# A gated loop and a feed-forward layer on one core: fp32 weight pieces, no selecting products for three pairs, and a new order table

## The chip, the core and the metric

The kernel runs on one core of a Trainium2 chip. A core has five engines that work in parallel and meet only through semaphores: PE (TensorE, matrix products), ACT (ScalarE), DVE (VectorE), POOL (GpSimd) and SP (SyncE, which here only issues DMA transfers). Each takes its instructions strictly in order. The metric is the device time of one execution in microseconds (us), as the median of several runs.

## The reference

There are 4 sequences of 768 steps with 8 heads of 48 columns. The first part is a linear attention whose state decays and turns by a complex gate a at each step. Its output, 384 columns a step, goes through a layer norm and a feed-forward layer:

```python
mag = np.sqrt(a_re * a_re + a_im * a_im)
scale = np.minimum(mag, 0.999) / (mag + 1e-06)
a_re_n, a_im_n = (a_re * scale, a_im * scale)
for t in range(S):
    new_re = ar * S_re - ai * S_im
    new_im = ar * S_im + ai * S_re
    kv = np.einsum('bhd,bhe->bhde', k[:, :, t], v[:, :, t])
    S_re, S_im = (new_re + kv, new_im)
    y[:, :, t] = np.einsum('bhd,bhde->bhe', q[:, :, t], S_re)
...
xn = (x - mu) / np.sqrt(var + 1e-06) * g_ln
ch = np.maximum(xn @ w_ch1, 0.0) @ w_ch2       # 384 -> 1536 -> 384
return (x + ch).astype(np.float32)
```

## The kernel before

**Tiling.** Steps are taken in chunks of 128, two chunks to a pair, so there are 12 pairs, three to a sequence. The pairs 0, 3, 6 and 9 are the first of their sequences. Pair 0 is done in two halves of four heads.

**Work of a pair.** From a_re and a_im come the logarithm of the gate's size (`ln`, `iv`, `r`, `r2`, `u`, `l`, `lc`) and its angle (`th`). Products with a triangle of ones (`u_e`, and `u_th`, which holds 1/2π) sum them over the steps: `dec` for the sizes, `ph` for the angles in turns. `e` and `en` are the exponentials of the sums; `sin` and `cos` come from the low 16 bits of the phase, with `abs` or `qt` on the way. `ke`, `ks`, `qe`, `qs` multiply k and q by them. `ksT` and `qsT` are their transposes: PE transposes into a bank and ACT or DVE copies it out, or SP does the whole with a transposing DMA. Then come the masked products within the chunk (`am`, `atm`), the state (`gm`, `gs`, `G`), the output `y`, the norm's figures (`bn`, `rstd`), the centred rows `x` and their transpose (`xtr`, `xT`), the feed-forward products `mm1`, `relu`, `mm2`, and the result `ot` (with `oa` where ACT takes a part of it), stored by `st`.

**Carried phase.** `ph` begins with a product of `pick`, a matrix that selects rows of `car`. `car` holds the phase at the end of the pair before it; for a sequence's first pair it is the constant 192 (`WINDOW`), which keeps the sum in a range whose low 16 bits are the fraction of a turn.

**Weights.** `wl.0` and `wl.1` are two casting DMAs from POOL's queue, each for a whole weight matrix (fp32 in memory, bf16 on the chip: `w1b`, `w2b`). `wc` then multiplies `w1b` in place by minus the norm's gain, in nine pieces of 512 columns, and `mm1` needs these, `mm2` needs `wl.1`.

**Order.** A long table, `PLAN`, written out by hand or by a planner, lists each step with its engine (P, A, V, G, S) and the PSUM bank. The kernel emits the steps in that order; the table is therefore each engine's order too. An `@` puts a step of POOL behind a step of DVE. The `warm` steps are products on `u_e` whose results nobody reads. `RINGS` gives the number of buffers of each kind: a step that writes a buffer waits for the readers of the step that many places before.

Of the kernel before, what the change touches and what calls it, by code (L numbers as in the profile page):

```python
# [20 lines left out]
TWO_PI_SAFE = 6.2831845  # L21
PSUM = bass.MemoryType.PSUM
# [15 lines left out]

OPTIONAL = ("kT", "qT", "xtr", "oa", "ac", "tab", "warm", "xr", "ks", "qs", "ke", "qe")
# [25 lines left out]
xtr.0:P4 kT.3:P6 ksT.2:V7 ph.2.0:P2 G.1:V0 qe.2.0.1:G@ksT.2 tab.trig.5:A th.3.0:A ksT.3:V6 am.2:P0 ngl:G@ksT.2
sin.2.0:A2 warm.w37:P7 v.1:G atm.2:V0 warm.13:P7 am.3:P6 xT.0:A4 qt.2.0:P2 r2.3.0:G@ksT.3 x.1:A5 gm.2:P4 atm.3:V6
ph.3.0:P0 cos.2.0:A2 xr.0:G G.2:V4 warm.23:P2 are.5.0:S xtr.1:P2 car.3.0:A0 warm.9:P3 warm.w41:P6 sin.3.0:A0 gm.3:P4
wc.0.1:V y.2:P7 wc.1.0:V y.3:P5 xT.1:A2 wc.1.1:V wc.1.2:V vf.2.0:S qt.3.0:P0 wl.1:G@wc.1.1 bn.2:V7 mm1.0.1.0:P2
cos.3.0:A0 wc.0.0:V mm1.0.1.1:P2 vf.2.1:S wc.0.2:V x.2:A7 wc.2.2:V mm1.0.0.1:P0 wc.2.0:V relu.0.1:A2 wc.2.1:V bn.3:V5
mm1.0.0.0:P0 qe.2.0.0:G@wc.2.1 xtr.2:P3 aim.5.0:S x.3:V5 mm1.0.2.0:P6 ke.2.0.0:G@bn.3 xT.2:V3 xtr.3:P5 mm1.0.2.1:P6  # L70
xT.3:V5 tab.log.6:A u.3.0:A gs.3:V4 mm1.1.0.1:P2 qs.2.0.0:V relu.0.2:A6 mm1.1.1.0:P4 ks.2.0.0:V relu.0.0:A0
mm1.1.1.1:P4 ks.2.0.1:V mm1.1.0.0:P2 l.3.0:V ln.4.0:A mm1.1.2.1:P0 relu.1.1:A4 relu.1.0:V2 kT.5:P6 mm1.1.2.0:P0
iv.4.0:A ksT.5:V6 qT.5:P4 relu.1.2:A0 lc.3.0:V qT.4:P3 r.4.0:G@ksT.5 qsT.5:V4 kT.4:P5 qsT.4:A3 dec.3.0:P6 ksT.4:V5
# [141 lines left out]
def kernel(  # L215
# [62 lines left out]
    def eng(name):  # L278
        return g.ops[name].eng
# [583 lines left out]
```

## Time and profile before

| what | value |
|---|---|
| device time, 3 runs | median 186.26 us (185.86 to 186.31) |
| span of the profiled execution | 184.4 us, from its first to its last instruction |
| that execution's own time | not given apart from the runs; 186.26 − 184.4 = 1.9 us lie around the span |
| busy: PE, DVE, ACT, POOL | 175.1, 154.5, 154.9, 111.2 us |
| of PE, warming products | 14.6 us (42 of 512 columns) and 7.1 us (29 of 256) |
| DMA | 35.39 MB in 128791 packets; SP's queue 84.3% and POOL's 7.0% of 16 engines' span |

A row of grouped instructions reads: line, engine, operation, output <- input, shape, count | busy us, mean ns of one | idle time of the engine before them and who ended it. PE's products are pipelined and their ends are modelled, so the durations of neighbours overlap and a busy PE need not be at its peak.

### The profile page before, as it was taken

To read this page: it belongs to the slowest core of one execution; us is meant where nothing else is said; L and a number is where in the kernel's file an instruction comes from. 1 tells how busy PE (TensorE), PEld (TensorE's weight loads), DVE (VectorE), ACT (ScalarE), POOL (GpSimd) and SP (SyncE) were. 2 spreads that over 40 slices of the span, in tenths; PEclk is the share of its full clock that TensorE was granted. 3 is DMA by queue.
4 is the path that set the end of the run, shared out by engine and by line. 5 is a ranking of instruction groups with operands and counts; after the bars stand their busy time and mean duration, and the time that the engine had idled before them with its cause. 6 is when DMAs were issued, how large, how long until landed. Compare 5 with 4: busy or idle time off the path is not lost.

```text
span 184.4 us, 5011 instructions
## 1 busy us (share of the span) xinstructions
PE 175.1 (95%) x1971; PEld 138.2 (75%) x1971; DVE 154.5 (84%) x273; ACT 154.9 (84%) x217; POOL 111.2 (60%) x124
## 2 busy tenths in 40 slices
PE   5968989999999999999999999999999999999992
PEld 2545367789866886987887897887977979788871
DVE  2349999998888999999989989988988999977431
ACT  5899988989999999999999999999989973466320
POOL 7484068942586847799799966877959530280000
PEclk9999999999999999999999999999999999999999
DMA  5999999999986999989896999989699999992302
GB/s 142 305 201 230 231 187 187 231 252 203 231 176 138 252 256 217 197 222 198 183 242 126 229 221 191 214 187 215 148 233 165 207 135 201 242 199 90 108 0 85
DMA packets 128791, 35.39 MB, mean 192 GB/s; under 512 B 124800, under 2 KB 128000, under 8 KB 128768
## 3 DMA queue, kind: packets, MB, share of 16 engines
q1 hardware_dynamic: 127968, 32.72, 84.3%
q0 software_dynamic: 800, 2.36, 7.0%
q8 instruction: 15, 0.25, 0.5%
q14 instruction: 8, 0.07, 0.1%
HBM read 28.31 MB, written 4.72 MB: 179 GB/s over the span
## 4 chain that ended last, share of the span: by engine, by line
PE 74%; DVE 10%; SPq 7%; DMA 4%; issue 2%; POOL 1%; DVEq 0%
PE banks L767 24%; PE banks L791 23%; PE banks L613 6%; PE banks L636 5%; SPq L452 3%; SPq L404 3%; PE banks L507 3%; PE banks L488 3%; PE banks L697 2%; PE banks L660 2%; PE banks L700 2%; DMA k<-in_k_dram 2%; PE banks L734 2%; DMA q<-in_q_dram 2%; DVE qs L295 1%
## 5 line engine op out<-in xcount | busy, mean ns | idle before, releaser
L791 PE MATMUL banks<-w2b,h 128*128 128x384 bf16 (+2 forms) x300 | 53.0, 319 | 0.1
L767 PE MATMUL banks<-xT,w1b 128*128 128x256 bf16 x432 | 51.5, 273 | 0.0
L767 PEld LDWEIGHTS <-w1b 128*128 128x128 bf16 x432 | 46.1, 114 | 1.1 <-DVE stats L707 0.3
L779 ACT ACTIVATE h<-banks 128x1024 bf16<-128x1024 f32 x31 | 31.5, 1021 | 11.5 <-PE banks L767 11.3
L791 PEld LDWEIGHTS <-h 128*128 128x128 bf16 x300 | 26.9, 97 | 13.8 <-issue 0.2
L295 DVE TENSOR_TENSOR atm<-banks,mask 128x1024 bf16<-128x1024 f32 x24 | 28.9, 1219 | 3.6 <-PE banks L636 3.3
L295 POOL TENSOR_TENSOR r<-aim,are 128x768 f16<-128x768 f32 x9 | 16.5, 1832 | 8.6 <-DVE ksT L292 7.5
L831 ACT ACT_TABLE_LOAD x15 | 19.2, 1283 | 1.0 <-PEq L847 0.8
L295 POOL TENSOR_TENSOR qe<-q,e 128x384 bf16<-128x384 f32 (+1 forms) x14 | 16.2, 1157 | 4.7 <-ACT e L492 1.7
L826 PE MATMUL banks<-u_e 128*128 128x512 f16 x42 | 14.6, 436 | 2.4 <-POOL u_e L323 2.2
L724 POOL TENSOR_SCALAR xr<-x,mv 128x384 f32<-128x384 bf16 x13 | 8.5, 653 | 11.0 <-ACT x L714 4.7
L707 DVE BATCH_NORM_STATS2 stats<-banks 128x6 f32<-128x384 f32 x24 | 13.3, 556 | 1.2 <-PE banks L700 1.2
L636 PE MATMUL banks<-qsT,ksT 128*128 128x128 bf16 x192 | 14.3, 219 | 0.0
L477 DVE SCALAR_TENSOR_TENSOR l<-r,w 128x768 f16<-128x768 f16 (+1 forms) x13 | 11.7, 907 | 2.6 <-ACT r L473 2.6
L807 DVE SCALAR_TENSOR_TENSOR ot<-banks,rstd,xr 128x384 f32<-128x384 f32 (+2 forms) x18 | 10.4, 586 | 3.9 <-PE banks L791 3.3
L636 PEld LDWEIGHTS <-ksT 128*128 128x128 bf16 x192 | 12.2, 97 | 1.6 <-DVE ksT L292 0.2
L414 POOL TENSOR_SCALAR v<-vf 128x768 bf16<-128x768 f32 x9 | 9.5, 1058 | 5.6 <-DVE mv L708 2.7
L805 POOL TENSOR_TENSOR ot<-ot,x 128x384 f32<-128x384 f32 x7 | 7.0, 1006 | 9.1 <-DVE atm L295 7.9
L697 PE MATMUL banks<-v,atm 128*128 128x48 bf16 x192 | 12.0, 183 | 0.2 <-DVE atm L295 0.2
L459 ACT ACTIVATE w<-are 128x768 f32<-128x768 f32 (+1 forms) x13 | 10.2, 791 | 2.2 <-DMA are<-in_a_re_dram 2.2
L295 POOL TENSOR_TENSOR ke<-k,en 128x768 bf16<-128x768 f32 (+1 forms) x9 | 11.8, 1321 | 0.2
L697 PEld LDWEIGHTS <-atm 128*128 128x128 bf16 x192 | 10.8, 96 | 1.4 <-DVE atm L295 0.6
(100 smaller groups left out, 391.0 us busy)
## 6 DMA issues: line engine op xcount, KB each, us to landing
vf<-in_v_dram SPq DMA_DIRECT2D x24, 192.0 KB, 3.0
q<-in_q_dram SPq DMA_DIRECT2D x24, 192.0 KB, 3.8
k<-in_k_dram SPq DMA_DIRECT2D x24, 192.0 KB, 3.8
out_dram<-ot SPq DMA_DIRECT2D x23, 192.0 KB, 2.3
are<-in_a_re_dram SPq DMA_DIRECT2D x8, 384.0 KB, 4.6
aim<-in_a_im_dram SPq DMA_DIRECT2D x8, 384.0 KB, 5.0
are<-in_a_re_dram SPq DMA_DIRECT2D x8, 192.0 KB, 4.7
aim<-in_a_im_dram SPq DMA_DIRECT2D x8, 192.0 KB, 3.8
```

The lines of the kernel that those rows point to most:

```text
L295: {"DVE": nc.vector, "POOL": nc.gpsimd}[eng(name)].tensor_tensor(**kw)
L477: nc.vector.scalar_tensor_tensor(out=S_("l"), in0=S_("r2"), scalar=0.5, in1=S_("w"), op0=ALU.mult, op1=ALU.add)
L613: nc.tensor.transpose(ps[:, h], T(nm, P)[:, c, h], ident)
L636: nc.tensor.matmul(ps[:, h], lhsT=T("ksT", n)[:, h], rhs=T("qsT", n)[:, h], start=True, stop=True)
L697: nc.tensor.matmul(ps[:, h], lhsT=T("atm", n)[:, h], rhs=T("v", P)[:, c, h], start=True, stop=nfirst)
L707: nc.vector.bn_stats(out=T("stats", n), in_=bank(f"y.{n}")[:, 0:DM])
L767: nc.tensor.matmul(ps[:, jj], lhsT=w1b[:, dc, ts(gi, JG * C)].rearrange("k (p j) -> k j p", j=JG)[:, jj], rhs=T("xT", P)[:, dc].rearrange( ...
L779: act(out=dst, in_=src, func=AF.Relu)
L791: nc.tensor.matmul(bank(f"o.{N}")[:, ws], lhsT=T("h", P)[:, j, ts(c, C)], rhs=w2b[:, j, ws], start=(j == 0), stop=(j == NJ - 1))
L807: nc.vector.scalar_tensor_tensor(out=o, in0=bank(f"o.{N}")[:, ws], scalar=T("rstd", P)[:, ds(c, 1)], in1=xs, op0=ALU.mult, op1=ALU.add)
L826: g.add(f"warm.w{i}", lambda i=i: nc.tensor.matmul(bank(f"warm.w{i}"), lhsT=u_e[:, 0, 0], rhs=u_e.rearrange("p c j t -> p (c j t)"), start ...
L831: g.add(f"tab.{nm}.{i}", lambda tab=tab: nc.scalar.preload_act_table_set(tab))
```

## The change

**Weights.** `wl.0` and `wl.1` are gone. SP issues 18 transfers of [128, 512] fp32 (`ws.0` to `ws.8` for w_ch1, `ws.9` to `ws.17` for w_ch2) into a ring of two buffers `ws`. Nine steps `wc` scale a piece into `w1b`, nine steps `wd` cast one into `w2b`. In the new table two `wc` and one `wd` are on DVE, two and two on ACT, five and six on POOL. `mm2` of a group of four row blocks needs the three pieces `wd` of that group.

**First pairs of sequences 1 to 3.** For pairs 3, 6 and 9, `ph` has no product of `pick`. A new step `root` writes 1206 (192 turns in radians, nearly) over the first step's angle instead, in one partition.

**Order table.** All of `PLAN` is new. Engines change with it: relu goes from 31 on ACT and 5 on DVE to 24 and 12, `oa` from 7 to none, ksT on ACT from none to 5, transposes of x by DMA from 2 to 6; the warming products become 60 of 512 columns and 9 of 256.

SP's queue, where the loads of pairs 4 to 6 stand (are, aim, k, q and vf are a_re, a_im, k, q and v; the number is the buffer). Before:

```order
L452 DMA are_65<-in_a_re_dram 128x8x96
L452 DMA aim_68<-in_a_im_dram 128x8x96
L452 DMA are_66<-in_a_re_dram 128x8x96
L404 DMA vf_76<-in_v_dram 128x8x48 x2
L452 DMA aim_69<-in_a_im_dram 128x8x96
L452 DMA are_64<-in_a_re_dram 128x8x96
L404 DMA q_70<-in_q_dram 128x8x48
L592 DMA row_166<-e_98 8x1x48
```

After:

```order
L401 DMA ws_168<-in_moe_w_ch_dram 128x512
L425 DMA vf_76<-in_v_dram 128x8x48 x2
L401 DMA ws_167<-in_moe_w_ch_dram 128x512
L473 DMA are_66<-in_a_re_dram 128x8x96
L401 DMA ws_168<-in_moe_w_ch_dram 128x512
L473 DMA are_64<-in_a_re_dram 128x8x96
L401 DMA ws_167<-in_moe_w_ch_dram 128x512
L473 DMA aim_69<-in_a_im_dram 128x8x96
L401 DMA ws_168<-in_moe_w_ch_dram 128x512
L473 DMA aim_67<-in_a_im_dram 128x8x96
```

The loads of are and aim of pairs 5 and 6 now stand between pieces of w_ch2, each of which waits for a cast.

ACT's queue around the last pair's exponentials (L492, then L513), which is where the first products of pair 8's feed-forward stand. Before:

```order
L831 ACT_TABLE_LOAD
L473 ACTIVATE r_88<-r_88 128x768
L290 COPY qsT_123<-banks 128x1024
L779 ACTIVATE h_158<-banks 128x1024
L714 ACTIVATE x_139<-banks,mv_149 128x384
L796 ACTIVATE ot_160<-banks,mv_147,rstd_152 128x384
L779 ACTIVATE h_158<-banks 128x1024 x2
L492 ACTIVATE e_98<-banks 128x768
L492 ACTIVATE en_100<-banks 128x768
```

After:

```order
L859 ACT_TABLE_LOAD
L778 ACTIVATE rstd_153<-mv_148 128x2
L779 ACTIVATE rstd_153<-rstd_153 128x2
L513 ACTIVATE e_98<-banks 128x768
L513 ACTIVATE en_100<-banks 128x768
L294 COPY ksT_116<-banks 128x1024
L742 ACTIVATE x_139<-banks,mv_149 128x384
L807 ACTIVATE h_158<-banks 128x1024 x2
```

The exponentials now stand ahead of pair 8's three relu (h_158), and a copy of ksT is ahead of them too.

PE's queue at the phase of pair 3 (th is the angle). Before:

```order
L503 LDWEIGHTS pick
L503 MATMUL banks<-car_164,pick 128x384
L507 LDWEIGHTS u_th
L507 MATMUL banks<-th_93,u_th 128x384
L507 LDWEIGHTS u_th
L507 MATMUL banks<-th_93,u_th 128x384
```

After:

```order
L534 LDWEIGHTS u_th
L534 MATMUL banks<-th_93,u_th 128x384
L534 LDWEIGHTS u_th
L534 MATMUL banks<-th_93,u_th 128x384
```

Each of the pair's two chunks has lost its product of `pick`. The code (of the table, one line of each; the rest is left out):

```diff
+ROOT_RAD = 1206.0
-         "mv": 5, "rstd": 5, "xT": 3, ...
+         "mv": 5, "ws": 2, "rstd": 5, "xT": 3, ...
+ROOT = {3, 6, 9}
...
-ue:G are.0.0:S are.1.0:S are.0.1:S uth:V aim.0.0:S warm.w27:P0 pad.ks.2:G warm.1:P0 aim.0.1:S pad.qs.2:G warm.w1:P7
+ue:G are.0.0:S aim.0.0:S car0.1:G uth:V warm.w0:P0 warm.w1:P0 one:G are.0.1:S zrow.0:G warm.w2:P0 zrow.1:G pad.qs.2:G
...
+              "row": ([C, HALF], BF16), "ws": ([C, 512], FP32), ...
...
-    g.add("wl.0", lambda: nc.gpsimd.dma_start(
-        out=w1b, in_=moe_w_ch1.rearrange("(dc p) j -> p dc j", p=C)))
-    g.add("wl.1", lambda: nc.gpsimd.dma_start(
-        out=w2b.rearrange("p (g j) e -> p g (j e)", j=JG),
-        in_=moe_w_ch2.rearrange("(g p j) e -> p g (j e)", p=C, j=JG)))
...
-    def f_wc(jb, ec):
-        w, sc, name = w1b[:, ec, ts(jb, 512)], ngl[:, ds(ec, 1)], f"wc.{jb}.{ec}"
-                out=w, in0=w, scalar1=sc, scalar2=None, op0=ALU.mult)
+    def f_wc(i, name, dst, sc):
         if eng(name) == "ACT":
+            nc.scalar.mul(out=dst, in_=T("ws", i), mul=sc)
         else:
+                out=dst, in0=T("ws", i), scalar1=sc, scalar2=None, op0=ALU.mult)
+    def f_wd(i, name, dst):
+        if eng(name) == "ACT":
+            nc.scalar.copy(out=dst, in_=T("ws", i))
+        else:
+                out=dst, in0=T("ws", i), scalar1=1.0, scalar2=0.0, op0=ALU.mult, op1=ALU.add)
+    for m in range(2):
+        for a in range(NG):
+            for b in range(ND):
+                i = (m * NG + a) * ND + b
+                src = w2d[:, a, ts(b, 512)] if m else moe_w_ch1[ts(b, C), ts(a, 512)]
+                g.add(f"ws.{i}", lambda i=i, src=src: nc.sync.dma_start(out=T("ws", i), in_=src),
+                      uses=[("ws", i)])
...
+            if P in ROOT:
+                def f_root(X=X, hs=hs, step=step):
+                    {"DVE": nc.vector, "POOL": nc.gpsimd}[eng(f"root.{X}")].memset(
+                        step(T("th", P), 0)[0:1], ROOT_RAD)
...
-                    nc.tensor.matmul(ps[:, c], lhsT=pick[rows], rhs=T("car", P)[rows, fs],
+                    if P not in ROOT:
+                        nc.tensor.matmul(ps[:, c], lhsT=pick[rows], rhs=T("car", P)[rows, fs],
...
-                                         start=False, stop=end,
+                                         start=(P in ROOT and j == 0), stop=end,
...
-                        needs=[f"relu.{P}.{part}", "wl.1"] + ...
+                        needs=[f"relu.{P}.{part}"] + [f"wd.{part}.{x}" for x in range(ND)] + ...
...
-    for i in range(29):
+    for i in range(9):
         g.add(f"warm.{i}", ...
-    for i in range(42):
+    for i in range(60):
         g.add(f"warm.w{i}", ...
```

More of the change, by code (lines that the diff above doesn't have):

```diff
@@ L65 @@
[L65 to L73, printed above, removed]
-are.6.0:S am.5:P0 e.3.0:A6 rstd.0:G am.4:P2 atm.5:V0 r2.4.0:A mm2.0.0:P4 mm2.0.1:P4 atm.4:V2 u.4.0:A q.3.0:S
@@ new lines @@
+mm1.2.0.1:P0 root.6.0:V st.2:S abs.5.0:V6 v.3:G@ks.3.0.0 q.5.1:S kT.7:P5 sin.5.0:A6 qs.3.0.0:V gm.6:P2 q.4.0:S kT.6:P4
+G.6:A2 mm1.2.0.0:P0 cos.5.0:A ksT.7:V5 v.4:G@qs.3.0.0 qT.7:P7 ksT.6:V4 relu.2.0:A0 qT.6:P6 ke.4.0.0:G@qs.3.0.0
+are.7.0:S qsT.7:V7 gm.7:P2 dec.5.0:P3 cos.4.0:A G.7:V2 am.7:P0 qsT.6:V6 r2.6.0:A vf.5.0:S ks.4.0.0:G mm2.4.0:P2
+atm.7:V0 am.6:P6 vf.5.1:S mm2.4.1:P2 atm.6:V6 y.7:P0 tab.log.8:A e.5.0:A3 aim.7.0:S mm2.5.0:P1 qe.4.0.0:G bn.7:V0
+en.5.0:A3 y.6:P6 mm2.4.2:P2 bn.6:V6 vf.6.0:S x.7:A0 gm.8:P7 ln.7.0:A ot.4:V2 xtr.7:P3 rstd.3:G kT.9:P5 k.5.0:S
```

205 lines of the change are left out of this document (110 added, 95 removed), and 2 rows, old and new, of the table RINGS.

## The prediction

> **What bounds the kernel now.** I read the page first, then three stretches, then the groups by shape, then the queues.
>
> ```profile
> span 184.4 us, 5011 instructions
> ...
> PE 175.1 (95%) x1971; PEld 138.2 (75%) x1971; DVE 154.5 (84%) x273; ACT 154.9 (84%) x217; POOL 111.2 (60%) x124
> ...
> ACT  5899988989999999999999999999989973466320
> ...
> PEclk9999999999999999999999999999999999999999
> DMA  5999999999986999989896999989699999992302
> ```
>
> The runs' median is 186.26 us, so 1.9 us lie around this execution's span; every sum below is a change of the span, carried over to the median. The clock is at nine tenths or more in every slice and leaves the sums. The slices say that ACT is as full as PE from 10 to 145 us and then nearly idle. So I cut the span at the first product of pair 0's feed-forward and at that of pair 8:
>
> ```profile
> 38.52 2.81 PE L767 MATMUL banks<-xT,w1b 128*128 128x256 bf16 x24
> ...
> 59.86 2.78 PE L767 MATMUL banks<-xT,w1b 128*128 128x256 bf16 x24
> ...
> 142.72 1.47 PE L767 MATMUL banks<-xT,w1b 128*128 128x256 bf16 x12
> ```
> ```profile
> 0.00:37.00 37.00, 31.31 (x278) 19.54 (x279) 27.31 (x51) 32.49 (x51) 22.90 (x40) 1.00 0.99 214
> 37.00:142.70 105.70, 105.65 (x1260) 86.56 (x1259) 97.36 (x175) 102.05 (x138) 78.43 (x73) 1.00 0.98 204
> 142.70:184.40 41.70, 38.18 (x437) 32.10 (x434) 29.83 (x49) 20.32 (x30) 9.88 (x12) 1.00 0.71 141
> ```
>
> The columns are the stretch, then PE, PEld, DVE, ACT, POOL, clock, share of the DMA engines, GB/s. In the middle PE lacks 0.05 us, ACT 3.6 us, DVE 8.3 us. In the last 41.7 us PE goes on alone and ACT is half idle. So PE is the bound after 37 us, but ACT stands 3.6 us behind it: an order that asks ACT for more than that before 142.7 us makes ACT the bound. ACT's one large wait, for the feed-forward's sums (11.3 us in all), lies mostly in the tail:
>
> ```profile
> ACT h L779 <- PE banks L767: 11.3, 14, 1.8
> ```
>
> **Selecting products gone.** Pairs 3, 6 and 9 lose two products each. Their pitch is the time to the next product, 0.16 us:
>
> ```profile
> 32.48 0.33 PE L503 MATMUL banks<-car,pick 128*128 128x384 f16 x1
> 32.65 0.49 PE L507 MATMUL banks<-th,u_th 128*128 128x384 f16 x2
> 32.97 0.33 PE L503 MATMUL banks<-car,pick 128*128 128x384 f16 x1
> ```
>
> 6 × 0.16 = 1.0 us off PE, on its busy part. Three fills of one row (root) come in, one on DVE and two on POOL, each like this one:
>
> ```profile
> L359 POOL MEMSET qrow<- 1x384 f16 x1 | 0.4, 411 | 0.1
> ```
>
> 0.4 us each on engines with idle time; nothing on the sum. The new order also drops 4 of 22 xtr groups of three 128-column products (by columns 4 × 0.16 = 0.6 us). PE's total falls by 1.6 us.
>
> **Weights.** The two casting transfers and the nine in-place scalings go; 18 pieces of 256 KB, nine scalings and nine casts from fp32 come.
>
> ```profile
> L385 DVE TENSOR_SCALAR w1b<-w1b,ngl 128x512 bf16<-128x512 bf16 x9 | 2.5, 345 | 0.0
> L724 POOL TENSOR_SCALAR xr<-x,mv 128x384 f32<-128x384 bf16 x13 | 8.5, 653 | 11.0 <-ACT x L714 4.7 <-DVE mv L708 1.7 <-DVE qe L295 1.7
> L414 POOL TENSOR_SCALAR v<-vf 128x768 bf16<-128x768 f32 x9 | 9.5, 1058 | 5.6 <-DVE mv L708 2.7 <-DVE xT L292 1.8 <-DVE ks L295 0.6
> L290 ACT COPY xT<-banks 128x384 bf16<-128x384 bf16 x6 | 2.9, 476 | 1.9 <-PE banks L734 1.8
> L412 ACT CAST v<-vf 128x768 bf16<-128x768 f32 x3 | 2.5, 822 | 0.0
> ```
>
> DVE keeps three pieces (0.345 each if fp32 costs nothing, 0.7 if it doubles; I take 0.5): 1.5 for the old nine's 2.5. POOL takes eleven, each between 0.65 and 1.06 us, by width 0.8: 8.8 us, which its 40% of idle time hides if the pieces are there. ACT takes four, between 0.48 and 0.82, by width 0.6: 2.4 us, with no cover, since ACT is full.
>
> **The moved work, on ACT.** Counting the table up to the first product of pair 8, with the mean of each kind:
>
> ```profile
> L779 ACT ACTIVATE h<-banks 128x1024 bf16<-128x1024 f32 x31 | 31.5, 1021 | 11.5 <-PE banks L767 11.3
> L542 ACT ACTIVATE sh<-banks 128x768 f16<-128x768 int16 x6 | 4.8, 808 | 0.0
> L796 ACT ACTIVATE ot<-banks,mv,rstd 128x384 f32<-128x384 f32 x7 | 4.7, 671 | 0.3 <-PE banks L791 0.3
> L290 ACT COPY dec<-banks 64x8 f32<-64x8 f32 x12 | 1.9, 156 | 0.6 <-PE banks L597 0.4
> L290 ACT COPY qsT<-banks 128x1024 bf16<-128x1024 bf16 x3 | 3.0, 1004 | 0.5 <-PE banks L613 0.5
> L714 ACT ACTIVATE x<-banks,mv 128x384 bf16<-128x384 f32 x14 | 8.0, 581 | 3.1 <-PE banks L700 2.4 <-DVE mv L708 0.5
> L750 ACT ACTIVATE rstd<-mv 128x2 f32<-128x2 f32 x2 | 0.4, 207 | 0.0
> L751 ACT ACTIVATE rstd<-rstd 128x2 f32<-128x2 f32 x2 | 0.4, 204 | 0.1
> L469 ACT ACTIVATE r<-r 128x768 f16<-128x768 f16 x5 | 4.2, 841 | 0.0
> L492 ACT ACTIVATE e<-banks 128x768 bf16<-128x768 f32 x11 | 8.8, 810 | 0.1
> L290 ACT CAST G<-banks 128x384 bf16<-128x384 f32 x3 | 1.4, 480 | 0.5 <-PE banks L660 0.5
> ```
>
> Gone from ACT before that point: 7 relu (7.15), 3 abs (2.42), 3 oa (2.01), 4 decay copies (0.62), together 12.2 us. Come to it: 5 ksT and 1 qsT (6.02), 5 x (2.90), 3 xT (1.43), 5 rstd at two instructions (2.06), 1 r2 (0.84), 1 e and 1 en (1.62), 1 G (0.48), 4 weight pieces (2.4), together 17.75. So 5.5 us more by durations. All ACT rows add up to 168 us for 154.9 busy, because neighbours overlap; so 5.1 us of time. Over the whole kernel ACT's sum is the same: it is pulled forward out of the idle tail. On DVE the same count gives:
>
> ```profile
> L781 DVE TENSOR_SCALAR h<-banks 128x1024 bf16<-128x1024 f32 x5 | 6.1, 1219 | 2.0 <-PE banks L767 1.9
> L292 DVE COPY ksT<-banks 128x1024 bf16<-128x1024 bf16 x16 | 10.9, 684 | 0.9 <-PE banks L613 0.5
> ```
>
> 7 relu (8.5), 5 G (2.8), 3 abs (2.9), 3 ot (1.8), 2 r (1.9) and smaller ones (4.4) come, 22.3 us; 5 ksT (3.4), 5 x (3.1), 7 scalings (2.1), 5 xT (1.8) and parts of ks, qs and ke (3.1) go, 13.5. That is 8.8 us more, 8.1 of time, against its 8.3 of slack: DVE has no cover left there either.
>
> **What PE still has to do from that point** shrinks by one y, four gm, one dec and two xtr groups. By columns, at 0.65 us for the 1536 of a dec group, that is 0.33 + 0.65 + 0.65 + 0.33 = 2.0 us:
>
> ```profile
> 48.69 0.65 PE banks L488 x4
> ```
>
> **The sum.** 5.1 − 2.0 = 3.1 us later, if ACT idles as before. At most its 3.6 us in the middle can be squeezed out, which gives −0.5; nothing squeezed and 3 us of new stalls (below) give +6. Since PE products still release much of ACT's work, I take half of the 3.6 as squeezed: 3.1 − 1.8 = +1.3. 186.3 + 1.3 = 187.6 us.
>
> **The start** is shorter and gives nothing by itself. ACT's count ahead of the first feed-forward product falls from 37.2 to 31.2, 5.5 us of time, so that product should run at about 33 instead of 38.5. But up to pair 2's first product, at 59.86 us in the old run, ACT's count is the same in both (+0.2 us: two relu, a sin, a cos, a car, an oa, an x and an xT fewer, two ksT, two rstd, a th and the four weight pieces more), and PE has done 0.6 us less of its own products by then: it fills up with 60 warming products of 512 columns and 9 of 256, where 42 and 29 stood (1.7 us more by columns). The early start is spent by then.
>
> **SP's queue.** The staging ring holds two pieces, so each piece waits for the cast of the piece two before it, and SP's later loads wait behind it. Durations to landing come from the view of the DMA issues:
>
> ```profile
> q<-in_q_dram SPq DMA_DIRECT2D x24, 192.0 KB, 3.8
> ...
> w1b<-in_moe_w_ch_dram POOLq DMA_DIRECT2D x1, 1152.0 KB, 10.1
> ```
> ```profile
> 36.08 0.74 SPq L452 DMA_DIRECT2D are<-in_a_re_dram  x1
> 36.87 2.80 SPq L404 DMA_DIRECT2D vf<-in_v_dram  x2
> 39.71 1.05 SPq L452 DMA_DIRECT2D aim<-in_a_im_dram  x1
> ```
>
> A piece needs about 0.5 issue, 3.8 landing (a 192 KB load's; the 1152 KB transfer's 10.1 would be 2.2 by bytes) and 0.75 cast: 5 us, two in flight. Thirteen pieces follow the load of pair 1's decay row at about 25 us, so 6.5 rounds or 33 us, to 58 us; with 2.2 us of landing, 22 us, to 47. ACT reaches its last cast after 56 us of counted work, about 55 us. Behind it stand a_re and a_im of pair 5: issued at 36.08 and 39.71 before, they now follow the tenth and twelfth of these pieces, at about 48 and 52 us. Bounds: 0 (47 us is early enough) to 3 us on ACT or DVE; I count 0 in the likeliest case, since the first stage's DMA engines were full (0.99) with the same bytes, and put the rest into a rival.
>
> [...]
>
> **Rivals.** (1) *PE sets the end and the early start is kept.* For it: PE has 1.6 us less to do, and the totals of ACT and POOL hardly grow. Against it: the count above. The removed 1.6 us of products less the 0.6 us that PE is behind at pair 2 give −1.0, 185.3 us; if of the 5.5 us by which the first product is earlier a fifth survives, another 1.1, −2.1. It decides if ACT idles under 0.5 us between 37 us and pair 8's first product. (2) *The ring of two stalls SP* and with it r2 and ln of pair 5: 1.3 + 2.5 = +3.8, 190.1 us. It decides if the last piece lands after 57 us. (3) *It comes out even:* the 1.0 us of products and the fuller ACT cancel, 186.3.
>
> **Chances.** Forecast 0.45, rival 1 0.27, rival 2 0.18, rival 3 0.10. This kernel's runs can tell about 0.3%, 0.56 us. Of the forecast's 0.45 some 0.08 fall within that; of rival 1's 0.27, 0.03 do; of rival 3's, 0.07, the rest is faster. So faster 0.27, same 0.18, slower 0.55. The likeliest case alone spans 186.4 to 189.3; the range over the cases, leaving out the ends of rivals 1 and 2, is 184.5 to 190.5.
>
> **What the new profile would show.** First feed-forward product at 32 to 35 us, and pair 2's near 60: the start is spent. ACT at 98% or more from 37 to 140 us and PE no longer full there: short waits of PE for h, x or ksT adding to 2 to 4 us. If PE lacks nothing after 40 us, rival 1 holds and my count of ACT is wrong. If SP waits on casts before the loads of pair 5 and ACT's ln or DVE's r2 wait more than a microsecond near 50 to 58 us, it is rival 2. No product of `pick` in pairs 3, 6 and 9. The prediction also fails if POOL, with eleven casts, delays r of pairs 3 and 4 by more than its idle time.

## The result: 200.3 us for 186.3, and the profile after

The changed kernel takes 200.33 us (median of 4 runs, 199.21 to 201.10), the kernel before 186.28 us: 1.0754 times as long, 95% interval 1.0723 to 1.0786. Foretold were 187.6 us and at most 190.5. In some executions of some kernels below the granted clock stood at 0.50 for a stretch, of an estimated 3.4 us or of 6.8 where it was profiled (figures in the last section); where that moves a number, the clock is told with it.

The page of the changed kernel, its span, totals, two rows of slices and the chain that ended last by engine:

```profile
span 198.9 us, 4986 instructions
...
PE 180.6 (91%) x1951; PEld 135.8 (68%) x1951; DVE 160.6 (81%) x263; ACT 155.0 (78%) x223; POOL 116.8 (59%) x117
...
PE   5999898869989989899998998989998998899993
...
ACT  4699898896998789989989977979999681545220
...
PE 28%; DVE 23%; ACT 14%; DMA 13%; POOL 12%; issue 5%; SPq 4%; DVEq 0%; POOLq 0%; ACTq 0%
```

The same row of the chain in the kernel before:

```profile
PE 74%; DVE 10%; SPq 7%; DMA 4%; issue 2%; POOL 1%; DVEq 0%
```

Before, the chain ran on PE for three quarters of the time. Now it changes between four engines and the DMA, and no engine is full: ACT's total is as it was (155.0 for 154.9), and its slices show eights and sevens where nines stood. PE's busy time rose by 5.5 us (175.1 before) with 20 products fewer in the trace: the 432 products of `mm1` have the same mean as before (273 ns) and cover 53.4 us where they covered 51.5, so neighbours overlap less, and a part of PE's waiting is counted as busy.

The first feed-forward product of pairs 0, 2 and 8, as the timeline of PE has them:

```profile
34.11 1.15 PE L795 MATMUL banks<-xT,w1b 128*128 128x256 bf16 x9
...
64.56 0.82 PE L795 MATMUL banks<-xT,w1b 128*128 128x256 bf16 x6
...
157.45 0.83 PE L795 MATMUL banks<-xT,w1b 128*128 128x256 bf16 x6
```

Pair 0 is 4.4 us earlier than before (38.52), pair 2 4.7 us later (59.86), pair 8 14.7 us later (142.72), and the end 14.5 us later. The busy time of the engines up to pair 2, from there to pair 8, and in the tail (columns as in the prediction: PE, PEld, DVE, ACT, POOL), first of the changed kernel, then of the one before:

```profile
0.00:64.56 64.56, 56.49 (x543) 37.06 (x544) 51.40 (x93) 55.59 (x83) 43.06 (x58) 1.00 0.92 225
64.56:157.45 92.89, 87.27 (x1024) 68.10 (x1024) 86.67 (x134) 84.33 (x121) 64.91 (x50) 1.00 0.99 201
...
157.45:198.90 41.45, 36.80 (x393) 30.64 (x388) 22.48 (x37) 15.05 (x20) 8.81 (x11) 1.00 0.57 120
```

```profile
0.00:59.86 59.86, 54.17 (x547) 38.38 (x548) 47.46 (x93) 54.68 (x80) 35.66 (x54) 1.00 0.96 209
59.86:142.72 82.86, 82.81 (x992) 67.72 (x990) 77.23 (x133) 79.88 (x109) 65.68 (x60) 1.00 0.99 205
```

Up to pair 8's first product ACT works 139.9 us (134.6 before, +5.4), DVE 138.1 (124.7, +13.4) and POOL 108.0 (101.3, +6.6). ACT's idle time there is 17.5 us, 8.2 before. So, counted by ACT, the 14.7 us are 5.4 us of added work, near the count, and 9.4 us by which ACT stands idle longer. The prediction had that second term at -1.8. Counted by DVE, the same 14.7 us are 13.4 us of added work and 1.35 us of added idle time (18.0 before, 19.4 now). Each is a sum over one engine; neither says which engine held up the others. In the middle the waits of ACT are for DVE, PE and POOL in turn, and PE waits for ACT and DVE (waits of the changed kernel, 64.56 to 157.45):

```profile
ACT trig L553 <- DVE sh L572: 3.8, 4, 1.4
ACT h L807 <- PE banks L795: 1.6, 3, 1.2
ACT e L513 <- PE banks L509: 1.2, 2, 0.8
ACT th L517 <- POOL r L299: 0.5, 1, 0.5
```

```profile
PE banks L795 <- ACT trig L553: 1.6, 2, 0.9
PE banks L641 <- DVE qs L299: 1.3, 2, 0.9
```

### The profile page after: what moved, and what is told of

It is laid out like the page before. It is cut to its first block, busy times and chain, and to the rows that moved or that the text cites. A ratio compares the mean times of both kernels' runs of the same rounds, so it can differ in the third digit from the quotient of the medians.

```text
span 198.9 us, 4986 instructions
## 1 busy us (share of the span) xinstructions
PE 180.6 (91%) x1951; PEld 135.8 (68%) x1951; DVE 160.6 (81%) x263; ACT 155.0 (78%) x223; POOL 116.8 (59%) x117
## 4 chain that ended last, share of the span: by engine, by line
PE 28%; DVE 23%; ACT 14%; DMA 13%; POOL 12%; issue 5%; SPq 4%; DVEq 0%; POOLq 0%; ACTq 0%
PE banks L819 10%; DMA aim<-in_a_im_dram 8%; PE banks L795 7%; PE banks L854 4%; DMA qsT<-qs 3%; DVE h L809 3%; ACT h L807 3%; ACT trig L553 2%; POOL ks L299 2%; DVE ot L835 2%; POOL qs L299 2%; ACT L859 2%; PE banks L641 2%; POOL w1b L386 2%; DVE sh L572 2%
## 5 line engine op out<-in xcount | busy, mean ns | idle before, releaser
L795 PE MATMUL banks<-xT,w1b 128*128 128x256 bf16 x432 | 53.4, 273 | 4.2 <-POOL w1b L386 2.1
L807 ACT ACTIVATE h<-banks 128x1024 bf16<-128x1024 f32 x24 | 24.3, 1021 | 10.9 <-PE banks L795 6.0
L299 POOL TENSOR_TENSOR ke<-k,en 128x768 bf16<-128x768 f32 (+1 forms) x10 | 15.4, 1545 | 10.2 <-DVE l L501 5.0
L752 POOL TENSOR_SCALAR xr<-x,mv 128x384 f32<-128x384 bf16 x18 | 12.9, 720 | 12.8 <-DVE ot L835 9.4
L835 DVE SCALAR_TENSOR_TENSOR ot<-banks,rstd,xr 128x384 f32<-128x384 f32 (+2 forms) x25 | 14.7, 594 | 6.7 <-PE banks L819 4.8
L809 DVE TENSOR_SCALAR h<-banks 128x1024 bf16<-128x1024 f32 x12 | 14.4, 1216 | 5.1 <-PE banks L795 5.1
L742 ACT ACTIVATE x<-banks,mv 128x384 bf16<-128x384 f32 x21 | 12.2, 579 | 8.2 <-DVE mv L736 8.2
L299 POOL TENSOR_TENSOR qe<-q,e 128x768 bf16<-128x768 f32 x9 | 14.9, 1650 | 2.6 <-DVE ks L299 2.6
L735 DVE BATCH_NORM_STATS2 stats<-banks 128x6 f32<-128x384 f32 x24 | 13.4, 556 | 3.6 <-PE banks L728 3.3
L299 POOL TENSOR_TENSOR r<-aim,are 128x768 f16<-128x768 f32 x7 | 12.7, 1817 | 3.2 <-DMA aim<-in_a_im_dram 1.9
L553 ACT ACTIVATE trig<-banks 128x768 bf16<-128x768 int16 (+1 forms) x13 | 9.9, 762 | 5.2 <-DVE sh L572 3.8
L299 POOL TENSOR_TENSOR ks<-ke,trig 128x1536 bf16<-128x1536 bf16 x4 | 12.4, 3100 | 2.2 <-DVE qs L299 1.4
```

Source lines behind the costliest of these rows:

```text
L299: {"DVE": nc.vector, "POOL": nc.gpsimd}[eng(name)].tensor_tensor(**kw)
L553: add(f"sin.{X}", lambda fs=fs, v16=v16: act(out=T("trig", P)[:, 1, :, fs], in_=v16(), func=AF.Sin, scale=TWO_PI_SAFE / TURN), needs=[f"ph ...
L735: nc.vector.bn_stats(out=T("stats", n), in_=bank(f"y.{n}")[:, 0:DM])
L752: {"DVE": nc.vector, "POOL": nc.gpsimd}[eng(f"xr.{n}")].tensor_scalar(out=T("xr", n), in0=T("x", n), scalar1=-1.0, scalar2=T("mv", P)[:, c ...
L795: nc.tensor.matmul(ps[:, jj], lhsT=w1b[:, dc, ts(gi, JG * C)].rearrange("k (p j) -> k j p", j=JG)[:, jj], rhs=T("xT", P)[:, dc].rearrange( ...
L807: act(out=dst, in_=src, func=AF.Relu)
```

## The experiments

Theories, by the letters of the expectations. A: the staged pieces cost the time (A' their loads on SyncE's queue). B: the order costs it. C, E: DVE, or ACT, is the bound in the middle. D: no engine is, the waits between the queues are. F: ACT and DVE together are overfull in the middle because the new order asks more of them there. G: the start leaves late stages behind that the middle inherits. H: the division of work among the engines. All ratios are to the kernel before, which ran on the same chip; the changed kernel's is 1.0754, and its spans are 197.5 to 199.4 us, at clocks of 0.997 to 1.000.

### The staging: ring, POOL's scalings, late loads, and none of it

**Four staging buffers.**

```diff
-"x": 10, ... "ws": 2, ... "gt": 2
+"x": 7, ... "ws": 4, ... "gt": 1
```

> The changed kernel with four staging buffers for the pieces in place of two; to make room the ring of x has seven buffers in place of ten and that of gt one in place of two. A piece's load then waits for the cast of the piece four before it. If SyncE's queue behind the ring carries the loss (rival 2 of the prediction), a_re and a_im of pair 5 come several us earlier and the time falls to 193 to 197 us. If the order carries it, the time stays at 199 to 201 us.

Measured 199.49 us, 1.0728 (1.0669 to 1.0787); three spans, at clocks of 0.999 and 1.000, are 196.5 to 198.0, about 1.2 us below the changed kernel's mean. The queue had the waits that rival 2 spoke of. SyncE's own, of the changed kernel, then two gate loads that stood behind pieces and the last piece:

```profile
SPq L401 <- POOL w2b L393: 4.2, 4, 1.6
...
SPq L401 <- DMA ws<-in_moe_w_ch_dram: 3.7, 3, 2.3
...
SPq L401 <- POOL w1b L386: 3.0, 3, 1.3
```

```profile
50.18 0.43 SPq L473 DMA_DIRECT2D are<-in_a_re_dram  x1
...
54.03 0.43 SPq L473 DMA_DIRECT2D aim<-in_a_im_dram  x1
...
56.02 0.34 SPq L401 DMA_DIRECT2D ws<-in_moe_w_ch_dram  x1
```

They are real and late (36.08 and 39.71 us before; 48 and 52 foretold). With four buffers these two loads are issued at 48.03 and 50.63, and most of the 14 us stays. The smaller rings of x and gt belong to this edit; from pair 3's first product to pair 8's it takes 73.8 us, the changed kernel 73.4, so they hide little there.

**Scaling by a constant.** The gain is left out of the slices that POOL and DVE scale.

```diff
-out=dst, in0=T("ws", i), scalar1=sc, scalar2=None, op0=ALU.mult)
+out=dst, in0=T("ws", i), scalar1=-1.0, scalar2=0.0, op0=ALU.mult, op1=ALU.add)
```

> The changed kernel, with the DVE and POOL scalings of the first weight by the constant -1 in place of the per-row gain (so the gain is left out of those slices; ACT's slices keep it). The instruction then has the form of the casts beside it, which take 0.62 us on POOL, against 1.6 us for the scalings. If POOL's slow scalings carry the loss of the start: five times 1.0 us less on POOL, PE's 2.1 us wait for w1b goes, and the time falls by 2 to 4 us, to 196 to 198 us. If the loss is made by the order, under 1 us: 199.5 to 200.5 us.

Measured 199.20 us, 1.0706 (1.0667 to 1.0746); spans 197.0 to 197.6, 1.1 us below. POOL's groups of the changed kernel, then the one of this run:

```profile
L386 POOL TENSOR_SCALAR w1b<-ws,ngl 128x512 bf16<-128x512 f32 x5 | 8.0, 1599 | 2.6 <-DVE qs L299 2.0 <-DVE ke L299 0.5
...
L393 POOL TENSOR_SCALAR w2b<-ws 128x512 bf16<-128x512 f32 x6 | 3.7, 617 | 6.0 <-DVE ks L299 2.8 <-DVE l L498 1.8 <-DMA ws<-in_moe_w_ch_dram 1.2
```

```profile
L386 POOL TENSOR_SCALAR w1b<-ws 128x512 bf16<-128x512 f32 x5 | 3.1, 616 | 3.4 <-DVE qs L299 2.0 <-DMA ws<-in_moe_w_ch_dram 0.9 <-DVE ke L299 0.5
```

POOL has 4.9 us less to do and the end comes 1.1 us earlier: POOL's price was wrong, but that carries only this 1.1 us.

**Earlier gate loads.**

```diff
-ws.11:S ... ws.10:S ... are.5.0:S ... aim.5.0:S
+are.5.0:S ws.11:S ... aim.5.0:S ws.10:S
```

> The changed kernel, with the loads of a_re and a_im of pair 5 moved forward on SyncE's queue, from behind the staged pieces 15 and 16 to ahead of pieces 11 and 10. Theory A' (the late gate loads behind the pieces make the 4.7 us by which pair 2's feed-forward is later than before, since the chain runs through the load of aim at 54 to 59 us): pair 2's first product at 61 to 62.5 us in place of 64.6, and 1 to 3 us off the end, 197 to 199 us. If the order of ACT and DVE sets it, pair 2 stays at 64 to 65 us and the end at 199.5 to 201 us.

Measured 201.88 us, 1.0851 (1.0830 to 1.0872), and pair 2 at 66.8 us, 2.3 later than unedited: both expectations missed. In the changed kernel the chain runs through the load of aim of pair 5, issued at 54.03 and landed 5.2 us later. Here that load is issued at 42.60, with four buffers at 50.63; in neither run does the chain pass through it, and pair 2 comes 2.3 us later and 0.9 us earlier. So A' carries at most about 1 us of the 4.7: other queues bind nearly as late.

**No pieces at all.** Twice, the new order with the two casting transfers of before. In the second, the first transfer is placed where the kernel before has it.

```diff
-ws.0 ... ws.17:S  wc.*.*  wd.*.*
+wl.0:G wl.1:G  wc.*.*:V in place      (first run: wl.0 after pick; second: after qs.0.0.0)
```

> The new order, the fills of one row and the dropped selecting products stay; the weights come as before, in two casting transfers on POOL's queue, and DVE scales the nine slices of the first in place. Gone are the 18 pieces, the eleven POOL, four ACT and three DVE casts and the ring of two on SyncE's queue. Theory A (the pieces: the ring of two, SyncE's queue behind it, and POOL's scalings of 1.6 us) says that most of the 14 us goes away: 186 to 190 us. Theory B (the order itself: work pulled forward on ACT and DVE, POOL's 3.1 us products in the chain, waits between queues that follow one another) says that most of it stays: 195 to 199 us.

> The new order with the weights as before (two casting transfers on POOL's queue, nine scalings on DVE, no pieces, no ring), the first transfer now issued after qs of pair 0 as in the kernel before, the second ahead of xr of the first chunk. First feed-forward product at about 36 to 38 us. If the order carries the loss up to pair 3: 198 to 203 us, with 48 to 50 us between pair 0's and pair 3's first products (36.7 before, 50.0 in the changed kernel). If the pieces carry the start's loss: 38 to 42 us between the two, 188 to 194 us.

Measured 207.0 us, 1.1120 (1.1067 to 1.1174), and 205.95, 1.1071 (1.1032 to 1.1110). Without the pieces the new order is slower still. In both a decay row lands late (in the first it takes 7.71 us in the chain; in the second PE stands 5.50 us for it, and the first product of pair 0 comes at 40.6 us), and a half-clock stretch follows (0.51 from 34.5 to 41.4 us, 0.50 from 34.5 to 37.5); but from pair 0's first product to pair 3's it is 49.4 us in the second run, 50.0 in the changed kernel, 36.7 before. So the new order is as slow there without the pieces. That doesn't show the pieces to be free at the start: these runs put all nine scalings on DVE, which in the second works 29.2 of the 30.2 us between pair 0's and pair 2's first products (26.6 of 30.5 in the changed kernel). For the middle A falls, by the rows further below; for the start it is left with the 1 us each that the ring and the scalings cost, and the rest is open.

### Which engine: none by itself

**Work moved between engines in the middle.** Three runs: five relu evictions from DVE to ACT, six x copies from ACT to DVE, four long products from POOL to DVE.

```diff
-relu.3.1:V0 relu.4.0:V0 relu.4.2:V6 relu.5.2:V4 relu.7.1:V0
+relu.3.1:A0 relu.4.0:A0 relu.4.2:A6 relu.5.2:A4 relu.7.1:A0
```

```diff
-x.6:A6 x.7:A0 x.8:A4 x.9:A3 x.10:A2 x.11:A7
+x.6:V6 x.7:V0 x.8:V4 x.9:V3 x.10:V2 x.11:V7
```

```diff
-ks.4.0.0:G ks.6.0.0:G@lc.7.0 qs.6.0.0:G ks.7.0.0:G@qs.7.0.0
+ks.4.0.0:V ks.6.0.0:V qs.6.0.0:V ks.7.0.0:V
```

> The changed kernel, with five of the seven relu evictions that DVE does between pair 2's and pair 8's feed-forward given to ACT (those named relu.3.1, 4.0, 4.2, 5.2 and 7.1; same place in the order): DVE loses 5 x 1.2 = 6.0 us there, ACT gains 5 x 1.02 = 5.1 us. Theory C (DVE is full in this stage: its rows add up to 93.8 us, 9.4 more than before, for a stage that grew by 10.0 us) says 3 to 6 us faster than the changed kernel: 194 to 197 us. Theory D (no engine is full; the stage is set by the waits between queues, POOL's 3.1 us products first) says within 1.5 us of it, 199 to 201.5 us. Theory E (ACT is the bound, as the prediction had it) says 3 to 5 us slower: 203 to 205 us.

> The changed kernel, with six normalizing copies (x of chunks 6 to 11) given from ACT to DVE, where before had them: ACT loses 6 x 0.58 = 3.5 us in the stage between pair 2 and pair 8, DVE gains 6 x 0.6 = 3.6 us. Theory C (DVE full): 3 to 4 us slower than the changed kernel, 203 to 204.5 us. Theory D (waits between queues): within 1.5 us of it. Theory E (ACT is the bound): 2 to 3.5 us faster, 196.5 to 198 us.

> The changed kernel, with four of POOL's long products (ks of pairs 4, 6 and 7, qs of pair 6; 3.1 us each on POOL) done by DVE at the same place in the order (0.95 us each), without their added waits: POOL loses 12.4 us, DVE gains 3.8 us. Theory D (POOL's long products in the chain set the stage): 3 to 8 us faster than the changed kernel, 192 to 197 us. Theory C (DVE is full): 2 to 4 us slower, 202 to 204 us.

Measured 202.75 us, 1.0890 (1.0858 to 1.0922); 202.61, 1.0893 (1.0843 to 1.0943); 201.81, 1.0851 (1.0803 to 1.0900). Pair 2 to pair 8 in the three runs, by windows:

```profile
67.21:161.97 94.76, 87.21 (x1025) 68.13 (x1024) 82.25 (x129) 87.99 (x126) 64.84 (x49) 1.00 0.97 191
```

```profile
65.89:159.33 93.44, 87.36 (x1024) 67.72 (x1022) 88.11 (x140) 81.65 (x115) 63.71 (x49) 1.00 0.99 199
```

```profile
64.13:158.44 94.31, 87.29 (x1024) 68.07 (x1025) 89.67 (x138) 83.99 (x121) 51.56 (x46) 1.00 0.98 198
```

(Of the six x copies, the kernel before has two on DVE, not all as the expectation says.) DVE is relieved by 4.4 us, or ACT by 2.7, or POOL by 13.4, and the stage of 92.9 us gets no shorter: it is 0.55 to 1.9 us longer, in one profile of each, where the changed kernel's own spans differ by 1.9. What C foretold of the first run (194 to 197 us), E of the second (196.5 to 198) and D of the third (192 to 197) stayed away. So C and E, each as the one bound, fall; of D, the part that blames POOL's long products falls too, and its 1.5 us around the changed kernel were passed in the first two runs (2.4 and 2.3 us). These two moved work to an engine that is nearly as full, so they say nothing of ACT and DVE together.

**Half of each relu.** In both kernels the evictions of pairs 2 to 8 copy half of their columns, so part of the feed-forward is left out.

```diff
+                if 2 <= P <= 8:
+                    dst, src = dst[:, 1:3], src[:, 1:3]
```

> The changed kernel, in which the relu evictions of pairs 2 to 8 copy only half of their columns (the other half of h keeps older values, so that part of the feed-forward is left out). Nothing else changes. Before pair 8's first product this takes some 0.4 us off each of about 11 on ACT and 0.55 off each of about 7 on DVE, 8.3 us from both together. Theory F (ACT and DVE together set the stage, at the 91% of both that they reach in it): 8.3 / 2 / 0.91 = 4.5 us off the middle, 195 to 197 us. Theory D (waits between queues, no engine): 1 to 2 us at most, 198.5 to 200 us.

> The same edit in the kernel before (relu of pairs 2 to 8 copies half of its columns, so part of the feed-forward is left out): 16 on ACT and 2 on DVE in the middle, 7.5 us less work. There PE lacks nothing between 37 and 143 us, so theory F gives 0 to 0.5 us: 185.5 to 186.5 us. If the time falls by 2 us or more, ACT and not PE set the pace of the kernel before, and the comparison with the changed kernel has to be read anew.

The changed kernel: 201.97 us, 1.0796 (1.0734 to 1.0858). One of its four executions, the profiled one, ran at a mean clock of 0.567 and took 300 us, so no stage can be read; the others have spans of 197.6 us at clock 0.998 and 200.0 and 200.5 at 0.989. Against some 198.5 that is 0.9 us less at best, where F foretold 4.5. F has no support here; for want of a clean profile I call it unsupported, not refuted. The kernel before: 186.04 us, 0.9994 (0.9972 to 1.0017), and in its middle

```profile
60.45:143.16 82.71, 82.65 (x991) 67.65 (x989) 76.50 (x133) 74.12 (x109) 65.78 (x60) 1.00 1.01 206
```

ACT is 5.8 us lighter (79.88 before), and PE still lacks 0.06 us. So ACT's work doesn't set that stage of the kernel before.

**The waits of POOL for DVE taken out.** All 42 marks `@` go (the kernel before has 54).

```diff
-wc.1.0:G@ke.0.0.0  r2.1.0:G@wc.0.0  v.3:G@ks.3.0.0  ...
+wc.1.0:G  r2.1.0:G  v.3:G  ...
```

> The changed kernel without the added waits that hold some POOL operations until a named DVE operation has ended; the order of every engine stays. If these waits make POOL late and so stretch the chain between the queues, the time falls by 2 to 6 us (194 to 198 us). If they keep POOL out of DVE's way, as the longer DVE operations beside POOL suggest (ks 1.06 us for 0.95 us), DVE's busy time rises by some us and the time stays or grows (200 to 204 us).

Measured 206.56 us, 1.1072 (1.1003 to 1.1142): the waits help. Two DVE groups, of the kernel before, the changed kernel, and this run:

```profile
L477 DVE SCALAR_TENSOR_TENSOR l<-r,w 128x768 f16<-128x768 f16 x11 | 10.7, 972 | 0.0
...
L480 DVE TENSOR_SCALAR l<-l 128x768 f16<-128x768 f16 x11 | 4.0, 367 | 0.0
```

```profile
L498 DVE SCALAR_TENSOR_TENSOR l<-r,w 128x768 f16<-128x768 f16 x11 | 11.7, 1073 | 0.1
...
L501 DVE TENSOR_SCALAR l<-l 128x768 f16<-128x768 f16 x11 | 5.4, 491 | 0.0
```

```profile
L495 DVE SCALAR_TENSOR_TENSOR l<-r,w 128x768 f16<-128x768 f16 x11 | 13.6, 1243 | 0.1
...
L498 DVE TENSOR_SCALAR l<-l 128x768 f16<-128x768 f16 x11 | 7.6, 687 | 0.0
```

The same DVE operation takes 0.37, 0.49 or 0.69 us in the mean. With no POOL work beside it, the second of the two takes 0.33 to 0.36 us in the kernel before and in the changed kernel; each one over 0.4 us (0.46 before; 0.48, 0.55, 0.66 and 1.29 changed) has POOL work beside it, though not each one beside POOL work is longer (0.35 to 0.38 before). What makes those longer isn't shown. The changed kernel already pays some of it in spite of its waits.

### The order: spliced, then taken apart

**Spliced orders.** Up to one point the one kernel's order, from there on the other's. Accumulator banks are chosen anew where the old number is still held, and what is begun ahead of the seam keeps its form.

```diff
 h420: changed order to  xr.5:G car.3.0:V3  | before's order from  sin.3.0:A3 qt.3.0:P3 cos.3.0:A3 st.2:S
 r416: before's order to ke.3.0.0:V ks.3.0.0:V | changed order from r.6.0:G dps.4:P5 decc.4:A5 xr.5:G
 h700: changed order to  G.13:V1 ksT.13:S   | before's order from  ph.8.0:P4 aim.10.0:S abs.8.0:A4 k.8.1:S
```

> A spliced order: up to pair 2's feed-forward the changed kernel's (with its staged pieces), from there on the order of before (engines, halves and places of its operations; root stays). Theory F (the middle is lost because the new order gives ACT and DVE together 15 us more to do between pair 2 and pair 8: their rows there add up to 93.8 + 82.9 us, before 84.4 + 77.2): the middle takes some 83 us again, and only the start's loss of 4.7 us stays: 188 to 192 us. Theory G (the start leaves late loads and late log stages behind, and the middle only inherits them): the middle stays at 90 us or more, 196 to 201 us.

> The splice the other way round: the order of before with its two casting transfers (and root) up to pair 2's feed-forward, from there on the changed kernel's order. Theory F: the start is as before (pair 2's first product at 60 us), the middle takes 91 to 94 us, 194 to 197 us. Theory G: the middle takes 83 to 85 us, 186 to 189 us.

> The changed kernel's order up to pair 5's feed-forward, from there on the order of before. In the changed kernel pair 5's first product is 9.8 us late, pair 8's 14.7 us. Theory F: the loss after the seam (4.9 us) goes away, 194.5 to 197 us. Theory G: it stays, 199 to 201 us.

Measured 196.28 us, 1.0547 (1.0513 to 1.0580); 197.85 us, of which three executions had a mean clock of 0.991 (in the profiled one the stretch is at the seam: eight tenths in the slices from 68.6 to 78.4 us) and one, at 1.000, took 194.72; 199.99, 1.0715 (1.0661 to 1.0768). Each seam costs some us of its own (in h420 pair 2 comes at 67.8 us), so the totals don't decide between F and G: those of h420 and h700 lie in G's bounds, the one of r416 at a clock of 1.000 in F's. Behind the seam, from pair 3's first product to pair 8's, the rows are clear. Before, changed, h420, r416, and the new order without pieces:

```profile
75.20:142.72 67.52, 67.47 (x814) 55.32 (x812) 62.76 (x107) 65.27 (x91) 55.61 (x52) 1.00 0.97 196
```

```profile
84.10:157.45 73.35, 69.27 (x813) 54.36 (x811) 68.80 (x103) 66.65 (x98) 52.31 (x40) 1.00 0.96 189
```

```profile
85.51:153.66 68.15, 67.41 (x809) 54.80 (x807) 63.67 (x106) 65.27 (x91) 56.09 (x53) 1.00 0.97 195
```

```profile
83.06:155.65 72.59, 68.94 (x814) 54.35 (x812) 68.00 (x103) 66.77 (x98) 50.81 (x39) 1.00 0.98 190
```

```profile
89.95:163.67 73.72, 69.30 (x814) 54.34 (x812) 69.00 (x103) 66.70 (x98) 52.54 (x40) 1.00 0.97 190
```

With the order of before this stretch takes 67.5 and 68.2 us, with the new one 73.4, 72.6 and 73.7, whatever came first and however the weights came. Behind h700's seam, from pair 5's first product to pair 8's, it takes 39.8 us, with a half-clock stretch in it (six tenths in the slice from 119.9 to 124.9 us), for 43.4 in the changed kernel and 38.4 before. So 5.8 of the 14.5 us belong to the new order of these pairs, engines included, which is shown; G falls. That the 8.9 us up to pair 3 (84.1 for 75.2) come with the new order too is argued from the run without the pieces, whose start is no shorter, and isn't shown apart from them.

**Places from one, engines from the other.** Every operation at the place in time of the one kernel, on the engine and in the form of the other.

```diff
 m1: before's sequence, with   ks.4.0.0:G relu.3.1:V x.7:A ksT.8:A ...   (engines and forms of the changed kernel)
 m2: changed sequence, with    ks.4.0.0:V relu.3.1:A x.7:V ksT.8:S ...   (engines and forms of the kernel before)
```

> The kernel before (its weights, root fills as in the run before), every operation at its old place in the order, but on the engine and in the form (halves or whole) that the changed kernel gives it; rstd alone stays where it was. Theory D (the loss is in the places in time: what one queue needs is now issued too close behind, or behind other work, on the other queues): 186 to 191 us. Theory H (the loss is in the division of the work: DVE's added relu, abs and r, POOL's 3.1 us products): 195 to 201 us.

> The other way round: the changed kernel (staged pieces, ring, root), every operation at its new place, but on the engine and in the form that the kernel before gives it; rstd and the pieces stay as changed. Theory D: 196 to 203 us. Theory H: 187 to 192 us.

Measured 234.17 us, 1.2564 (1.2494 to 1.2634), and 225.20 us, 1.2056 (1.2000 to 1.2112). Pair 2 to pair 8 in the two:

```profile
71.30:181.26 109.96, 89.36 (x973) 67.82 (x972) 86.75 (x125) 80.52 (x111) 66.56 (x55) 0.96 0.84 165
```

```profile
71.02:180.06 109.04, 90.97 (x1031) 69.20 (x1030) 89.28 (x142) 84.57 (x119) 62.26 (x56) 0.98 0.80 170
```

Both theories miss by 22 us or more. The engines' busy time is near that of the changed kernel, yet the stage is 16 to 17 us longer than there and 26 to 27 longer than before (at a clock of 0.96 and 0.98): places and engines are fitted to each other, and neither half can be blamed by itself. That ACT, DVE, PE and POOL each wait on others is shown; which few places of the new order begin it stays open.

### The part that should have paid: the selecting products

```diff
+root.3.0:G root.6.0:G root.9.0:G     (first run: each right behind th; second: 6 and 9 just ahead of their use)
-nc.tensor.matmul(ps[:, c], lhsT=pick[rows], ...)   in pairs 3, 6 and 9
```

> The kernel before, with one part of the change alone: the row of each sequence's first pair is filled (root, on POOL, behind the arctangent of pairs 3, 6 and 9) and the selecting products of these pairs are dropped; weights and the rest of the order stay. The prediction's term for this: 1.0 us less on PE, 185.3 us in the units of 186.3 before. Rival: nothing, within 0.5 us of before, since the products were cover for something else; or 0.5 to 1 us slower, if the fill comes late on POOL's queue and the angle sums of the pair wait for it.

> The kernel before with the root fills and without the selecting products of pairs 3, 6 and 9, as in the run before, but with the fills of pairs 6 and 9 later in POOL's order (just ahead of their use), so that POOL doesn't stand waiting for the arctangent. If that wait cost the 0.7 us by which pair 6 came later: 185.0 to 185.7 us, faster than before by the 1.0 us of products. If the products were worth nothing: 186.0 to 186.7 us.

Measured 186.71 us, 1.0040 (1.0021 to 1.0059), and 186.40 us, 1.0014 (0.9993 to 1.0034). In the second run PE has 173.8 us of work for 175.1 before, and in the middle

```profile
59.74:142.83 83.09, 82.49 (x987) 67.31 (x986) 77.44 (x133) 79.89 (x109) 66.26 (x62) 1.00 1.00 208
```

it now lacks 0.6 us of 83.09 where it lacked 0.05. The removed work turned into waits. Taking PE's work away gains nothing, taking ACT's away (the half relu) gains nothing. This fits an order in which each stands right behind the other; no run takes away both at once.

## Why the prediction was wrong, by its steps

- **The sum is the step that failed, in its term for ACT's idle time.** "I take half of the 3.6 as squeezed" gave -1.8; ACT's idle time up to pair 8's first product rose from 8.2 to 17.5 us, +9.4. The count of loads assumed that the waits before and after are alike, or shorter. They belong to an order, and the order was new: the chain of waits left PE for all the queues. That this comes with the new order is shown from pair 3 to pair 8 and argued ahead of it; which places of the order make the waits stays open.
- **ACT's moved work** was counted right: +5.1, measured +5.4. **DVE's** was not: +8.1 counted, +13.4 measured, about 2.5 of it, over the kernel, because the two steps of l take longer (11 x 0.10 and 11 x 0.12 us). The 8.1 were set against "its 8.3 of slack", and the sentence that DVE "has no cover left there either" had no term in the sum. The slack covered nothing: between pair 2 and pair 8 DVE does 9.4 us more and stands idle 6.2 us, 5.6 before. POOL's +6.6 was called hidden.
- **"The early start is spent by then"**: the first product came at 34.1 us as foretold (32 to 35), pair 2 not near 60 but at 64.56. Only ACT had been counted (+0.2, measured +0.9); DVE does 3.9 us and POOL 7.4 us more ahead of that point. The early pair 0 left work behind it: from its first product to pair 2's the stage grew from 21.3 to 30.5 us, and in it ACT has 27.3 us of work for 20.9, DVE 26.6 for 18.7 and POOL 21.5 for 12.3.
- **PE left after pair 8**: -2.0 foretold; PE's work in the tail fell by 1.4 (36.80 for 38.16), the tail by 0.2 us. With 14.7 this makes the 14.5 us.
- **Selecting products**: 1.3 us did come off PE's work when done alone, and nothing off the time.
- **Weights**: DVE's pieces cost 0.50 and 0.42 us (0.5 foretold); POOL's scalings 1.60 and casts 0.62 where 0.8 stood for both, 11.7 us for 8.8. The pieces land in 3.3 us in the median, 3.0 to 5.1 (3.8 foretold), and the gate loads behind them were 2 us later than foretold.
- **Rivals**: the ring of two did stall SyncE's queue, and the last piece, issued at 56.02 us, landed behind rival 2's mark of 57; but neither ACT's ln nor DVE's r2 waits more than a microsecond between 50 and 58 us, two more buffers gave back about 1.2 us, not 2.5, and 12 were lost elsewhere. Rivals 1 and 3 fall. That the sign was right is in part luck: ACT's added work is a third of the size, and no run shows that it cost time (ACT relieved of 2.7 us gained none).
- **The signs foretold**: ACT at 98% or more was wrong (91% in the middle); PE's short waits did appear: between pair 2 and pair 8 it lacks 5.6 us (0.05 before) in place of 2 to 4, and the stage is 10.0 us longer. PE's total was to fall by 1.6 us; its busy time rose by 5.5.

## What to carry to other kernels

Where several in-order queues feed each other and two of them are nearly full, a change of the order can't be priced by adding up one engine's work: the waits are part of the order. Here ACT, taken for the bound, got 5.4 us of work and 9.4 us of new waits. Idle time is no cover until a run shows it: DVE's 8.3 us were counted as slack, and DVE kept its idle time and ran longer by its added work. Read the chain by engine first: where it left the bounding engine, the load sums of ACT (5.4) and DVE (13.4) both stayed below the 14.7 us. Such a table is fitted as a whole: moving, lightening or re-timing single entries of it changed nothing or cost time in every run here but the two that took a known extra cost out (about 1 us each).

## What the runs showed of the hardware that was not expected

A POOL scaling by a per-row operand takes 1.60 us for 128x512 from fp32 to bf16, the same by a constant 0.62; on DVE the two differ by 0.08 us (0.50 and 0.42, of two instructions and one).

At some holes in PE's work the clock dropped to half. In the new order with old weights (second run) PE stands for 5.50 us, and the clock is then 0.50 for a stretch; PE's row behind the hole, and three windows:

```profile
34.53 0.21 PE L605 MATMUL banks<-ident,row 8*64 8x8 bf16 x1 [5.50 <-DMA row<-e]
```

```profile
29.00:34.50 5.50, 0.03 (x1) 0.00 (x0) 1.21 (x4) 0.12 (x1) 2.78 (x1) 0.96 1.05 221
34.50:37.50 3.00, 2.97 (x35) 2.20 (x36) 1.69 (x4) 2.62 (x6) 1.12 (x1) 0.50 1.11 301
37.50:41.00 3.50, 2.85 (x41) 2.43 (x39) 3.24 (x11) 2.33 (x4) 1.44 (x2) 1.00 1.21 282
```

By these windows the stretch lasts an estimated 3.4 us (all 3.0 of the second, and 5.50 x 0.04 x 2 = 0.4 of the first). In the run without the waits of POOL the clock is 0.50 from 124.40 to 131.20 us, at a hole of 2.66 us; the profiled half relu in the changed kernel has a mean clock of 0.567 over 298.7 us. Holes of 1.46 to 2.12 us had such a stretch behind them in some runs and none in others:

- 2.12 us up to the product at 41.80, in the changed order up to pair 5: six tenths in the slice from 40.0 to 45.0 us. 2.10 us up to the product at 41.20, in the changed kernel: 1.00 from 41 to 48 us.
- 1.46 us and then 0.90 up to the product at 67.82, in the changed start with the old rest: six tenths in the slice from 68.3 to 73.2 us. 1.46 us up to the product at 122.21, with the four products off POOL: nine tenths or more in every slice.

What decides between the two isn't shown. At half the clock for 3.4 us PE loses at most an estimated 1.7 us; the 24 products at 67.82 take 4.45 us, 24 of the kernel before (at 59.86) 2.78.
